# Batch 0's first pair: a mix's copies behind the second product, w_out's decoding behind the mix's step, v's second part one step at a time from group 3

## The chip, the cores and the metric

The kernel runs on one core of one Trainium2 chip. The metric is the device time of one execution in microseconds (us); a profiled execution's span runs from its first to its last instruction. TensorE is called PE, VectorE DVE, ScalarE ACT, GpSimd POOL and SyncE SP.

## The reference

Two stages follow each other. Channel attention over two batches of 6016 tokens and 256 channels: q and k are normalized over the tokens, `s = knᵀ qn / tau` is a 256 x 256 matrix for each batch, `a = softmax(s)`, and the result is `v @ a`. Then a feed-forward layer over all 12032 tokens, with 2048 hidden channels:

```python
    h = x @ w_in
    g = h * (1.0 / (1.0 + np.exp(-h)))
    return (g @ w_out).astype(np.float32)
```

## The kernel before

The kernel multiplies `a` into `w_in` first, one mixed weight for each batch, so that the hidden layer is a product of this weight with v. Each fp32 operand is split into two fp16 halves, hi and lo, and a product is made of three matmuls (lo x hi, hi x lo, hi x hi).

**Pairs and groups.** A *pair* is 1024 tokens (896 at a batch's end), in two halves of 512: six pairs per batch, twelve in all. In each pair there are eight *groups* i = 0..7, each for 256 of the 2048 hidden channels. A group would need eight products of 512 columns; by a Strassen-Winograd scheme `emit_pair_group` does it in seven, in three PSUM banks: y and x (L657 on), z, then y, x, x, x again. Between them ACT copies a bank (`copy`, L640: c5 and c1, then c2), DVE subtracts (`minus`, L645: g11, g12, g22), ACT applies silu (L651, the fourth straight from the last x), and `finish` splits the result into hl: ACT casts the high half (L147), DVE makes the low half (L148). The generator yields four times in a group, in *slots* 0 to 3: behind z, behind the second x, behind the third x, behind the last x.

**Output matmuls.** Each of the four hl of a group gives six output matmuls into bank o (`emit_out`, L595). They are issued a group late, one hl per slot, as the list `pending`. A pair's last ones are followed by the evictions of its four o banks (L614 on ACT, L618 on DVE), and the next pair's output matmuls take the same four banks.

**The mixed weights.** Group i's weights are wall[i], made by `mix(b, i)`: 12 matmuls into bank w (L419), two scaled copies on ACT (L427), three subtractions on DVE (L433, L437, L440), then a cast to the high half on ACT (L144) and the low half on DVE (L145). The first matmul of a group's first y reads the low half. In pair 0, wall[i+1] is made during group i, one step of the generator per slot (`nextmix`), and before it `decode_wi` decodes w_in's next part (L186 on ACT, L188 on DVE, split by L147 and L148).

**Other work in pair 0.** `prepare`, in groups 0 and 1, goes on with `prepare_out`, which loads, decodes (L182 on POOL, L186, L188) and bounds (L196) w_out, and with two steps of batch 1's scores (`sc`, L277). Until w_out's scale is there, group 2 is not issued. `scale_v(1)` prepares the second pair's v: two squares (L481), the scale, and fp16 sums of v's halves in tile m (ACT L147, DVE L148, 1024 columns at once where they can be).

**What sets the order.** Instructions are emitted with a priority (their place in the program) and the tile framework orders each engine's list. `mark` notes the last instructions emitted, and `background` puts what it emits behind those on ACT, DVE and PE. Each engine works its list off in order.

```python
                mark()
                if p == 0 and i < NI - 1:
                    nextmix = background(nextmix)
```

Of the kernel before, what the change touches and what calls it, by code (L numbers as in the profile page):

```python
# [30 lines left out]
def channel_attention_then_silu_ffn(ctx, tc, kq, qT, kT, vT, tau, w_in, w_out, outT):  # L31
# [43 lines left out]
    def small_psum(name):  # L75

        if early[0]:
            return ps_o.tile([P, 512], F32, tag="o", name=name)
        return ps_b.tile([P, 512], F32, tag="z", name=name)
# [61 lines left out]
    def split(src, hi, lo, s=None):  # L141

        if s is None:
            nc.scalar.copy(hi, src)  # L144
            nc.vector.tensor_tensor(out=lo, in0=src, in1=hi, op=ALU.subtract)  # L145
            return
        nc.scalar.activation(out=hi, in_=src, func=AF.Copy, scale=s)  # L147
        nc.vector.scalar_tensor_tensor(  # L148
            out=lo, in0=src, scalar=s, in1=hi, op0=ALU.mult, op1=ALU.subtract
        )  # L150
# [261 lines left out]
    def mix(b, i):  # L412

        aT, rows = mixer[b]
        w = small_psum("w") if b == 0 else ps_b.tile([P, 512], F32, tag="a", name="w")
        for cb in range(KC):
            for j, (u, y) in enumerate(((1, 0), (0, 1), (0, 0))):
                for db in range(KC):
                    nc.tensor.matmul(  # L419
                        w[:, cb * C : (cb + 1) * C], aT[:, u, db, cb * P : (cb + 1) * P],  # L420
                        wi[:, y, db, i * C : (i + 1) * C],
                        start=(cb + db + j == 0), stop=(j == 2 and db == KC - 1),
                        skip_group_check=True,
                    )
        x = st.tile([P, 8, P], F32, tag="sq", name="x", bufs=2)
        for cb in range(KC):
            nc.scalar.activation(  # L427
                out=x[:, cb : cb + 3 : 2],
                in_=w[:, cb * C : (cb + 1) * C].rearrange("p (a c) -> p a c", c=P),
                func=AF.Copy, scale=rows[:, cb : cb + 1],  # L430
            )
        yield
        nc.vector.tensor_tensor(  # L433
            out=x[:, S1 : S3 + 1], in0=x[:, A21 : A21 + 1].to_broadcast([P, 2, P]),
            in1=x[:, A22 : A11 + 1], op=ALU.subtract,
        )
        nc.vector.tensor_tensor(  # L437
            out=x[:, S2], in0=x[:, S1], in1=x[:, A11], op=ALU.subtract
        )
        nc.vector.tensor_tensor(out=x[:, S4], in0=x[:, S2], in1=x[:, A12], op=ALU.add)  # L440
        yield
        m = wall[:, i]
        for a, c in ((A22, S3), (S3, S4 + 1)) if b or i == 0 else ((A22, S4 + 1),):
            hi, lo = m[:, 0, a - 1 : c - 1], m[:, 1, a - 1 : c - 1]
            if b:
                nc.vector.tensor_copy(out=hi, in_=x[:, a:c])
                nc.vector.tensor_tensor(out=lo, in0=x[:, a:c], in1=hi, op=ALU.subtract)
            else:
                split(x[:, a:c], hi, lo)
            yield  # L450
        mixed[b, i] = m


    pairs = [(b, n, min(NT, N - n)) for b in range(B) for n in range(0, N, NT)]
    loaded, parts = {}, {}

    def load_v(p):
        if p >= len(pairs):
            return
        b, n, w = pairs[p]  # L460
        t = vp.tile([P, KC, NT], F32, tag="v", name="v_t", bufs=3)
        nc.sync.dma_start(
            t[:, :, :w], vT[:, b * N + n : b * N + n + w].rearrange("(k p) n -> p k n", p=P)
        )
        loaded[p] = t
# [219 lines left out]
    def steps(gen):  # L685

        while True:
            try:
                next(gen)
            except StopIteration as e:  # L690
                return e.value

    def spend(gen, n=1):
        for _ in range(n):
            if gen is None:
                return None
            try:
                next(gen)
            except StopIteration:
                return None  # L700
        return gen
# [71 lines left out]
    def traced():  # L773
        return nc.cur_bb.bb.instructions
# [13 lines left out]
    def behind(start, those, engines=GATED):  # L788

        for i in traced()[start:]:  # L790
            if i.engine in engines and i.engine in those:
                tc.add_manual_dep(
                    i, those[i.engine].name,
                    mybir.DependencyInfo(
                        mybir.DependencyClass.NoSync, mybir.DependencyReason.DATA
                    ),
                )
# [10 lines left out]
    with at(0):  # L808
# [11 lines left out]
        for g in range(len(groups[0])):  # L820
# [15 lines left out]
            if g == 9:  # L836
                vgen = scale_v(0)
# [16 lines left out]
    def mark():  # L854

        anchor.update(last_of())

    def background(gen, n=1):

        start = len(traced())  # L860
        gen = spend(gen, n)
        behind(start, anchor)
        return gen

    def decode_wi(j):
        x = yield from decode(None, raws[j])
        while "in" not in weights:
            yield
        split(x, *(wi[:, u, :, j * C : (j + 1) * C] for u in range(2)), weights["in"][0])
# [58 lines left out]
    def prepare():  # L928

        nonlocal filler  # L930
        for _ in range(2):
            if "out" not in weights:
                next(wout)
        filler = spend(filler, 2)
# [5 lines left out]
    for p, (b, n, w) in enumerate(pairs):  # L940
        vgen = None
        last = n + w == N and b + 1 < B
        if n + w == N - pairs[-1][2] and b + 1 < B:
            steps(sqgen)
            norms["go"] = True
        for i in range(NI):
            if i == (4 if p == 0 else 0) and p + 1 < len(pairs):
                load_v(p + 1)
                vgen = scale_v(p + 1)
            if p == 0:  # L950
                if i == 2:
                    while "out" not in weights:
                        prepare()
                    spend(wout)
                    early[0] = False
                if i < NI - 1:
                    for j in ((), (2,), (3,), (4, 5), (6, 7), (), ())[i]:
                        steps(decode_wi(j))
                    nextmix = mixes.pop(0)
            if b and (b, i) not in mixed:  # L960
                steps(mixes.pop(0))
            pending, ready[:] = ready[:], []
            if p == 0 and i == 1:
                held_back = pending
                pending = []
            if p == 0 and i == 2:
                pending = held_back + pending
            slot = 0
            for _ in emit_pair_group(p, i):
                if p == 0 and i < 2:  # L970
                    prepare()
                take = 2 if p == 0 and i > 2 and len(pending) > 4 - slot else 1
                for _ in range(take):
                    if pending:
                        emit_out(pending.pop(0))
                mark()
                if p == 0 and i < NI - 1:
                    nextmix = background(nextmix)
                if i >= 1 and vgen is not None and (
                    p == 0 or slot in ((0, 2) if not last else (0, 2, 3) if i > 4 else (2, 3))  # L980
                ):
                    vgen = background(vgen, 2 if p == 0 else 1)
                if filler is not None and b == 0 and (p or i >= 2):
                    if "go" not in norms or slot < 2:
                        filler = background(filler, 1)
                if p in (1, 2, 3) and sqgen is not None and slot == 1:
                    sqgen = background(sqgen) or iter(())
                if p and mixes and slot == 0:
                    if mixes[0] is old and background(mixes.pop(0), 2):
                        raise RuntimeError("a mix has more steps")  # L990
                if p and mixes and slot != 1:
                    old = mixes[0]
                    background(old)
                if p == 0 and 2 <= i < 5 and slot in (0, 2):
                    wout = background(wout)
                slot += 1
            if last:
                mixes.append(mix(b + 1, i))
            ready[:0] = pending
            if p == 0 and i < NI - 1:  # L1000
                if nextmix is not None:
                    steps(nextmix)
        if vgen is not None:
            steps(vgen)
# [32 lines left out]
```

## Time and profile before

| | |
|---|---|
| Runs, median of 3 | 1035.51 us (1035.3 to 1035.76) |
| The profiled execution | 1035.6 us, span 1033.8 us |
| PE busy | 1026.4 us, 99% of the span |
| ACT busy | 836.2 us, 81% |
| DVE busy | 716.2 us, 69% |
| POOL busy | 9.8 us, 1% |
| HBM read, written | 57.67 MB, 12.32 MB |

The profiled execution stands 1.8 us above its span, and within the runs' spread. Busy matmuls are pipelined, so that PE's 99% says that it seldom lacks work, not that it runs at its peak. Pair 0 begins at 63.3 us of the span, behind the loading of k and q, and its eight groups last until 176 us.

### The profile page before, as it was taken

The numbers are of one execution on the slowest core, as the hardware profiler recorded it, in microseconds if no ns is written. First come the engines' busy times: TensorE is split into PE (matmuls) and PEld (weight loads), VectorE is DVE, ScalarE is ACT, GpSimd is POOL, SyncE is SP. The second block draws the span as 40 slices with busy tenths as digits, with TensorE's granted clock in tenths as the row PEclk, the third lists the DMA queues.
The fourth block names the chain that finished last, engine by engine and source line by source line (L and its number), as shares of the span: only waits on it lengthen the run. The fifth ranks groups of instructions, "written<-read, shape, count | busy, mean of one in ns | idle before, by whom it ended". The sixth has DMA issues, their size and how long they took to land.

```text
span 1033.8 us, 13058 instructions
## 1 busy us (share of the span) xinstructions
PE 1026.4 (99%) x4942; PEld 519.7 (50%) x4942; DVE 716.2 (69%) x1229; ACT 836.2 (81%) x1342; POOL 9.8 (1%) x23
## 2 busy tenths in 40 slices
PE   9999999999999999999999999999999999999998
PEld 8877554444444444444555444444444444444554
DVE  5987676667667667767688767667667667667654
ACT  6677788889989889788778778778778778778876
POOL 1011000000000000000000000000000000000000
PEclk9999999999999999999999999999999999999999
DMA  9996420312313101100101100200200100100101
GB/s 371 396 399 207 131 85 38 102 42 94 100 45 98 60 1 40 43 1 22 62 1 42 36 1 1 82 1 1 77 1 1 41 1 1 41 1 0 42 1 36
DMA packets 25984, 70.82 MB, mean 69 GB/s; under 512 B 2498, under 2 KB 3650, under 8 KB 25922
## 3 DMA queue, kind: packets, MB, share of 16 engines
q1 hardware_dynamic: 25346, 68.84, 18.8%
q8 instruction: 38, 0.62, 0.3%
q10 hardware_dynamic: 432, 0.64, 0.2%
q0 software_dynamic: 144, 0.52, 0.1%
q14 instruction: 24, 0.20, 0.1%
HBM read 57.67 MB, written 12.32 MB: 68 GB/s over the span
## 4 chain that ended last, share of the span: by engine, by line
PE 89%; DVE 4%; ACT 3%; DMA 2%; issue 1%; DVEq 0%; SPq 0%; ACTq 0%
PE o L595 45%; PE x L634 22%; PE y L634 11%; PE z L634 5%; PE sc L277 4%; DMA kq_t<-in_kq 2%; PE w L419 1%; DVE wo L274 1%; DVE hl L148 1%; ACT g L651 1%; ACT hl L147 1%; DVE g L645 1%; PE idle L815 0%; ACT m L147 0%; ACT c L640 0%
## 5 line engine op out<-in xcount | busy, mean ns | idle before, releaser
L595 PE MATMUL o<-hl,wo 128*128 128x512 f16 (+1 forms) x2304 | 548.7, 375 | 0.0
L148 DVE SCALAR_TENSOR_TENSOR hl<-g,sg,hl 128x512 f16<-128x512 f32 (+1 forms) x384 | 282.5, 739 | 172.2 <-ACT hl L147 170.5
L595 PEld LDWEIGHTS <-wo 128*128 128x128 f16 x2304 | 225.5, 98 | 261.2
L634 PEld LDWEIGHTS <-wall 128*128 128x128 f16 x2016 | 196.6, 98 | 226.7 <-issue 3.0
L634 PE MATMUL x<-m,wall 128*128 128x512 f16 (+1 forms) x1152 | 306.2, 375 | 1.0 <-ACT c L640 0.7
L651 ACT ACTIVATE g<-g,alpha 128x512 f32<-128x512 f32 (+1 forms) x288 | 203.5, 707 | 118.2 <-DVE g L645 116.9
L147 ACT ACTIVATE hl<-g,sg 128x512 f16<-128x512 f32 (+1 forms) x384 | 271.5, 711 | 10.3
L634 PE MATMUL y<-m,wall 128*128 128x512 f16 (+1 forms) x576 | 153.1, 375 | 0.5 <-DVE wall L145 0.5
L640 ACT COPY c<-x 128x512 f32<-128x512 f32 (+1 forms) x192 | 110.6, 576 | 24.8 <-PE x L634 21.5
L645 DVE TENSOR_TENSOR g<-x,c 128x512 f32<-128x512 f32 (+1 forms) x96 | 65.2, 680 | 45.2 <-PE x L634 45.2
L645 DVE TENSOR_TENSOR g<-c,z 128x512 f32<-128x512 f32 (+1 forms) x96 | 64.9, 676 | 38.4 <-PE z L634 33.7
L277 PE MATMUL sc<-kq_t 128*128 128x256 f32 x376 | 86.9, 384 | 0.0
L645 DVE TENSOR_TENSOR g<-c,y 128x512 f32<-128x512 f32 (+1 forms) x96 | 64.7, 674 | 18.7 <-ACT c L640 18.4
L277 PEld LDWEIGHTS sc<-kq_t 128*128 128x128 f32 x376 | 71.5, 193 | 11.4 <-DMA kq_t<-in_kq 0.3
L634 PE MATMUL z<-m,wall 128*128 128x512 f16 (+1 forms) x288 | 76.5, 375 | 0.0
L651 ACT ACTIVATE g<-x,alpha 128x512 f32<-128x512 f32 (+1 forms) x96 | 63.4, 661 | 1.3 <-PE x L634 1.3
L640 ACT COPY c<-y 128x512 f32<-128x512 f32 (+1 forms) x96 | 54.7, 569 | 8.7 <-PE y L634 6.9
L147 ACT ACTIVATE m<-v_t,sv 128x512 f16<-128x512 f32 (+2 forms) x46 | 33.1, 726 | 3.9 <-DVE sv L123 3.0
L274 DVE TENSOR_TENSOR wo<-wo,sq 128x1024 f32<-128x1024 f32 (+1 forms) x24 | 27.7, 1156 | 10.3 <-ACT sq L272 9.2
L148 DVE SCALAR_TENSOR_TENSOR m<-v_t,sv,m 128x512 f16<-128x512 f32 (+2 forms) x46 | 34.7, 758 | 0.0
L148 DVE SCALAR_TENSOR_TENSOR m<-x,sv,m 128x512 f16<-128x512 f32 (+2 forms) x35 | 26.2, 753 | 8.7 <-ACT m L147 8.7
L272 ACT ACTIVATE sq<-kq_t 128x1024 f32<-128x1024 f32 (+1 forms) x24 | 23.6, 998 | 7.6 <-DMA kq_t<-in_kq 4.8
(132 smaller groups left out, 396.0 us busy)
## 6 DMA issues: line engine op xcount, KB each, us to landing
kq_t<-in_kq SPq DMA_DIRECT2D x39, 512.0 KB, 8.2
v_t<-in_vT SPq DMA_DIRECT2D x10, 1024.0 KB, 5.1
outT<-sb SPq DMA_DIRECT2D x40, 256.0 KB, 2.1
turned<-in_qT SPq DMA_DIRECT2D x10, 512.0 KB, 3.6
turned<-in_kT SPq DMA_DIRECT2D x10, 512.0 KB, 3.5
kq_t<-in_kq SPq DMA_DIRECT2D x14, 256.0 KB, 7.4
raw<-in_w_in SPq DMA_DIRECT2D x5, 512.0 KB, 9.8
wo<-in_w_out SPq DMA_DIRECT2D x4, 512.0 KB, 9.6
```

Of the source, the lines that this page charges most:

```text
L147: nc.scalar.activation(out=hi, in_=src, func=AF.Copy, scale=s)
L148: nc.vector.scalar_tensor_tensor(out=lo, in0=src, scalar=s, in1=hi, op0=ALU.mult, op1=ALU.subtract)
L272: nc.scalar.activation(out=sq[:, :n], in_=t[:, :n], func=AF.Square)
L274: nc.vector.tensor_tensor(out=a, in0=a, in1=sq[:, :n], op=ALU.add)
L277: nc.tensor.matmul(sc[:, cb, :], t[:, i, 0, cb * P : (cb + 1) * P], t[:, i, 1, :], start=(j + i == 0 and cb == 0), stop=(j + i == J - 1), ...
L419: nc.tensor.matmul(w[:, cb * C : (cb + 1) * C], aT[:, u, db, cb * P : (cb + 1) * P], wi[:, y, db, i * C : (i + 1) * C], start=(cb + db + j ...
L595: nc.tensor.matmul(o[:, :h], a[:, f, ee], hl[:, m, :h], start=(c == 1 and i == 0), stop=(c == NF and i == 2),)
L634: nc.tensor.matmul(bank[:, :h], wm[:, u, a - 1], m[:, y, x, :h], start=(first and j == 0), stop=(j == 2), skip_group_check=True,)
L640: nc.scalar.copy(t[:, :h], bank[:, :h])
L645: nc.vector.tensor_tensor(out=g[:, :h], in0=a[:, :h], in1=c[:, :h], op=ALU.subtract)
L651: nc.scalar.activation(out=g[:, :h], in_=src[:, :h], func=AF.Silu, scale=alpha)
```

## The change

Four edits, all of them for batch 0, and in pair 0 alone in effect. A mix with i > 0 gets one more yield, between its 12 matmuls and its copies: the copies come in slot 1, the subtractions in slot 2, the split in slot 3. `prepare` comes behind the mix's step, no longer ahead of the output matmuls. The load and the scaling of pair 1's v begin in group 3, not 4. Its steps come one at a time in slots 0, 2 and 3, not two at a time in every slot.

```diff
@@ -422,6 +422,8 @@
                         start=(cb + db + j == 0), stop=(j == 2 and db == KC - 1),
                         skip_group_check=True,
                     )
+        if b == 0 and i:
+            yield
         x = st.tile([P, 8, P], F32, tag="sq", name="x", bufs=2)
         for cb in range(KC):
             nc.scalar.activation(
@@ -944,7 +946,7 @@
             steps(sqgen)
             norms["go"] = True
         for i in range(NI):
-            if i == (4 if p == 0 else 0) and p + 1 < len(pairs):
+            if i == (3 if p == 0 else 0) and p + 1 < len(pairs):
                 load_v(p + 1)
                 vgen = scale_v(p + 1)
             if p == 0:
@@ -967,8 +969,6 @@
                 pending = held_back + pending
             slot = 0
             for _ in emit_pair_group(p, i):
-                if p == 0 and i < 2:
-                    prepare()
                 take = 2 if p == 0 and i > 2 and len(pending) > 4 - slot else 1
                 for _ in range(take):
                     if pending:
@@ -976,10 +976,12 @@
                 mark()
                 if p == 0 and i < NI - 1:
                     nextmix = background(nextmix)
-                if i >= 1 and vgen is not None and (
-                    p == 0 or slot in ((0, 2) if not last else (0, 2, 3) if i > 4 else (2, 3))
+                if p == 0 and i < 2:
+                    prepare()
+                if i >= 1 and vgen is not None and slot in (
+                    (0, 2, 3) if p == 0 or last and i > 4 else (2, 3) if last else (0, 2)
                 ):
-                    vgen = background(vgen, 2 if p == 0 else 1)
+                    vgen = background(vgen, 1)
                 if filler is not None and b == 0 and (p or i >= 2):
                     if "go" not in norms or slot < 2:
                         filler = background(filler, 1)
```

How the engines' lists move is shown at three places; from L425 on, a line of the changed kernel has a number higher by two.

**ACT, the end of group 0**, before and then changed. `x<-w,rows` are the mix's copies, `wall<-x` is the mix's cast, `g<-x,alpha` the silu of the last x, `t<-wo` and `t<-wall` are decoding casts for w_out.

```order
L427 ACTIVATE x<-w,rows 128x2x128 x2
L640 COPY c_634<-x 128x512
L186 CAST t<-wo 128x512
L651 ACTIVATE g<-g,alpha 128x512
L147 ACTIVATE hl<-g,sg 128x512
L651 ACTIVATE g<-g,alpha 128x512
L147 ACTIVATE hl<-g,sg 128x512
L144 CAST wall<-x 128x896
L651 ACTIVATE g<-x,alpha 128x512
L186 CAST t<-wall 128x512
L147 ACTIVATE hl<-g,sg 128x512
```

```order
L642 COPY c_631<-x 128x512
L429 ACTIVATE x<-w,rows 128x2x128 x2
L186 CAST t<-wo 128x512
L653 ACTIVATE g<-g,alpha 128x512
L147 ACTIVATE hl<-g,sg 128x512
L653 ACTIVATE g<-g,alpha 128x512
L147 ACTIVATE hl<-g,sg 128x512
L653 ACTIVATE g<-x,alpha 128x512
L186 CAST t<-wall 128x512
L147 ACTIVATE hl<-g,sg 128x512
L144 CAST wall<-x 128x896
```

The cast into wall stood ahead of the last x's silu; now it stands behind it, behind a decoding cast and behind the last hl cast. The mix's copies stand behind c2.

**DVE, the end of group 6**, before and then changed. `wall<-x,wall` is the low half of wall[7], `m<-v_t,sv,m` belongs to pair 1's v.

```order
L645 TENSOR_TENSOR g<-c_1431,y 128x512
L148 SCALAR_TENSOR_TENSOR hl<-g,sg,hl 128x512
L433 TENSOR_TENSOR x<-x 128x256
L437 TENSOR_TENSOR x<-x 128x128
L440 TENSOR_TENSOR x<-x 128x128
L645 TENSOR_TENSOR g<-x,c_1387 128x512
L148 SCALAR_TENSOR_TENSOR hl<-g,sg,hl 128x512
L145 TENSOR_TENSOR wall<-x,wall 128x896
L148 SCALAR_TENSOR_TENSOR hl<-g,sg,hl 128x512 x2
```

```order
L647 TENSOR_TENSOR g<-x,c_1375 128x512
L148 SCALAR_TENSOR_TENSOR hl<-g,sg,hl 128x512
L435 TENSOR_TENSOR x<-x 128x256
L148 SCALAR_TENSOR_TENSOR m<-v_t,sv,m 128x1024
L439 TENSOR_TENSOR x<-x 128x128
L442 TENSOR_TENSOR x<-x 128x128
L148 SCALAR_TENSOR_TENSOR hl<-g,sg,hl 128x512 x2
L525 TENSOR_TENSOR x<-x,v_t 128x512
L145 TENSOR_TENSOR wall<-x,wall 128x896
L647 TENSOR_TENSOR g<-c_1476,z 128x512
```

Wall's low half stood ahead of the group's last two hl; now it stands behind them, behind a low half of v over 1024 columns (which before stood in group 5) and behind a subtraction for v.

**PE, group 7 from its z on**, before and then changed, with buffer numbers: `m_293` is pair 0's v, `wall` the weights, `o_886<-hl_1422` an output matmul for group 6's first hl.

```order
L634 MATMUL z_1490<-m_293,wall_87 128x512
L634 LDWEIGHTS wall_87
L634 MATMUL z_1490<-m_293,wall_87 128x512
L595 LDWEIGHTS wo_86
L595 MATMUL o_886<-hl_1422,wo_86 128x512
L595 LDWEIGHTS wo_86
L595 MATMUL o_886<-hl_1422,wo_86 128x512
L595 LDWEIGHTS wo_86
```

```order
L636 MATMUL z_1482<-m_293,wall_87 128x512
L636 LDWEIGHTS wall_87
L636 MATMUL z_1482<-m_293,wall_87 128x512
L636 LDWEIGHTS wall_87
L636 MATMUL y_1471<-m_293,wall_87 128x512
L636 LDWEIGHTS wall_87
L636 MATMUL y_1471<-m_293,wall_87 128x512
L636 LDWEIGHTS wall_87
```

Before, group 6's output matmuls stood between z and the second y. Now they stand ahead of group 7: counted over the list, 168 output matmuls come before group 7's first product, and 144 before. Behind z the second y follows at once.

## Rows read from the trace of the kernel before

**Rows 1.** The page: busy times, and the granted clock in tenths over 40 slices.

```profile
PE 1026.4 (99%) x4942; PEld 519.7 (50%) x4942; DVE 716.2 (69%) x1229; ACT 836.2 (81%) x1342; POOL 9.8 (1%) x23
PEclk9999999999999999999999999999999999999999
```

**Rows 2.** Timeline of PE, 60 to 165 us: start us, us, instruction, count [idle before, releaser].

```profile
65.25 1.03 PE L277 MATMUL sc<-kq_t 128*128 128x256 f32 x4
...
73.34 0.81 PE L634 MATMUL x<-m,wall 128*128 128x512 f16 x3
73.98 2.75 PE L277 MATMUL sc<-kq_t 128*128 128x256 f32 x12
77.21 0.82 PE L634 MATMUL y<-m,wall 128*128 128x512 f16 x3 [0.47 <-DVE wall L145]
...
92.58 0.22 PE L98 MATMUL pb<-spread,ones 128*128 128x128 bf16 x1
...
96.14 0.81 PE L634 MATMUL y<-m,wall 128*128 128x512 f16 x3
...
98.08 1.46 PE L595 MATMUL o<-hl,wo 128*128 128x512 f16 x6
99.38 1.47 PE L419 MATMUL w<-wi,aT 128*128 128x256 f16 x12
```

**Rows 3.** Timeline of ACT, v's cast at 150 us and the pairs' change at 181 us.

```profile
150.28 1.15 ACT L147 ACTIVATE m<-v_t,sv 128x1024 f16<-128x1024 f32 x1
...
181.16 1.06 ACT L242 ACTIVATE sq<-turned 128x1024 f32<-128x1024 f32 x1
...
182.21 0.71 ACT L651 ACTIVATE g<-g,alpha 128x512 f32<-128x512 f32 x1
...
186.55 0.68 ACT L614 ACTIVATE sb<-o,back 128x512 f32<-128x512 f32 x1
187.12 0.58 ACT L640 COPY c<-y 128x512 f32<-128x512 f32 x1
```

**Rows 4.** Timeline of DVE, groups 0 and 1.

```profile
65.15 0.75 DVE L148 SCALAR_TENSOR_TENSOR wi<-t,swi,wi 128x512 f16<-128x512 f32 x1 [0.72 <-ACT wi L147]
...
75.47 0.68 DVE L196 TENSOR_REDUCE ao<-wall 128x1 f32<-128x512 bf16 x1
76.07 1.08 DVE L145 TENSOR_TENSOR wall<-x,wall 128x896 f16<-128x896 f32 x1
...
85.27 0.28 DVE L93 TENSOR_SCALAR spread<-ident,ao 128x128 bf16<-128x128 f32 x1
```

**Rows 5.** Timeline of ACT, the end of group 0.

```profile
74.64 0.92 ACT L144 CAST wall<-x 128x896 f16<-128x896 f32 x1
75.47 0.68 ACT L651 ACTIVATE g<-x,alpha 128x512 f32<-128x512 f32 x1
76.05 0.77 ACT L186 CAST t<-wall 128x512 f16<-128x512 bf16 x1
76.67 0.72 ACT L147 ACTIVATE hl<-g,sg 128x512 f16<-128x512 f32 x1
```

**Rows 6.** Timeline of DVE, v's sums in group 5.

```profile
151.35 0.68 DVE L523 TENSOR_TENSOR x<-x,v_t 128x512 f32<-128x512 f32 x1
...
152.16 1.28 DVE L148 SCALAR_TENSOR_TENSOR m<-v_t,sv,m 128x1024 f16<-128x1024 f32 x1
```

**Rows 7.** Timeline of PE: group 7's first y, pair 1's first output, group 2 of pair 1.

```profile
166.23 0.81 PE L634 MATMUL y<-m,wall 128*128 128x512 f16 x3
...
187.60 1.46 PE L595 MATMUL o<-hl,wo 128*128 128x512 f16 x6
...
195.37 0.81 PE L634 MATMUL y<-m,wall 128*128 128x512 f16 x3
```

**Rows 8.** Waits of PE over the span: us in total, times, longest us.

```profile
PE idle L815 <- DVE ones L53: 1.1, 1, 1.1
PE x L634 <- ACT c L640: 0.7, 2, 0.4
```

## The prediction

> **What bounds the kernel now.** I read the page's busy times first, then the windows of 10 us, then the timeline of each engine from 60 to 202 us, where everything the change moves stands. The page shows TensorE (PE) busy for 99% of the span, ScalarE (ACT) for 81%, and the granted clock at its upper level, 2.4 GHz, in every slice [rows 1]. So a microsecond is lost or won only where PE waits. In the timeline of PE the reader sees matmuls that start one behind the other: a product of three matmuls takes 0.65, six output matmuls 1.30, twelve of a mix 1.31, twelve score matmuls 2.59 [rows 2] (a row's length less 0.16, which is its drain: 73.34, 0.81 long, next 73.98). The wait that the change is about is at 77.21, the first product of group 1, which waited 0.47 for the low half of wall[1] [rows 2].
>
> I call the seven products of a group by their banks: first y, first x, z, second y, second x, third x, last x. I compare three legs between first products: group 0 to group 2, group 2 to group 7, group 7 to group 2 of the next pair. On each, I take the new order of the three engines and put to each instruction the duration of its row; one that starts behind another follows after about 0.1 less than the row's length (186.55, 0.68 long, next 187.12) [rows 3]. PE's matmuls are the same in kind and number, so the sum is one of waits.
>
> **Leg 1, group 0 to group 2: +1.3 us.** In group 0 two edits cancel. The mix's 12 matmuls now follow z at 65.25 without the score matmuls ahead of them, and wait for the low half of wi, done at 65.90 [rows 2, 4]: they end 0.46 late. The third x no longer waits for its copy behind the two mix copies, which gives about as much back. So the last x stands where it stood, at 73.34 [rows 2]. From there the new order on ACT is: silu of the last x, a decoding cast, the hl cast, and only then wall's cast, which before ran ahead of that silu, at 74.64 [rows 5]. The result is there at 74.15; the third x, issued at 70.93, has its subtraction done by 72.89 and its silu by 73.65, so ACT is at its hl cast until 74.30; silu 74.30 to 74.97; cast from 74.87; hl cast 75.49 to 76.21; wall's cast 76.11 to 77.03. On DVE two reductions (0.60 each) and the low half of hl (0.66, the kind of 65.15) come first, until 77.46, then wall's low half, 1.08 [rows 4], ends at 78.54. PE's cover is the last x and 12 score matmuls: until 76.57 [rows 2]. So the first y comes at 78.56, not 77.21: +1.35. All of PE's list is queued behind this y, and ACT's next copy waits for its result. In group 1 the same walk finds wall[2] ready at 92.7, while score matmuls last until 97.4 (before: 96.14 [rows 2]); nothing more is lost, and 1.28 stays. Decoding of w_out moves behind the mix's step: casts, reductions and DVE's merges come up to one step later, its DMAs stand where they stood on SP and POOL, and POOL's memsets keep their order. I cost this at nothing because its end, the spread of w_out's bound at 85.27, has until the matmul pb at 92.58 [rows 2, 4]; without that cover each step is 0.6 to 0.7 us. Bounds of the leg: if the reductions run while DVE would idle, 0.9; if a cast waits for its memset, 2.0.
>
> **Leg 2, groups 2 to 7: +1.9 us.** The first y of each group now waits for a chain that starts at the last x before it: 0.81 to the result, silu 0.7, a decoding cast 0.62 in groups 2 and 3, hl cast 0.72, wall's cast 0.92, wall's low half 1.08. The order lets PE run score matmuls and output matmuls meanwhile, taken from the next group's share. From the last x: group 2, chain 4.68 against a cover of 0.65 + 1.30 + 0.86 + 8 x 0.216 = 4.53; group 3, 4.69 against 4.53; group 4, 4.96 against 0.65 + 17 x 0.216 = 4.32, since the third x's subtraction and the bits of v's scale stand in the way; group 5, 6.38 against 0.65 + 25 x 0.216 = 6.05, with v's cast over 1024 columns (1.15) and its low half (1.28) ahead of wall's two [rows 3, 6]; group 6, 6.5 against 0.65 + 20 x 0.216 = 4.97, with the same v cast ahead of the third x's silu, and v's subtraction (0.68 [rows 6]) ahead of wall's low half. These waits are 0.15, 0.16, 0.64, 0.33 and 1.53, together 2.8; in group 4 v's two squares hold up the copy of the first x, 0.2: 3.0. Before, the leg took 70.09 (96.14 to 166.23) [rows 2, 7], and its matmuls take 35 x 0.648 + 144 x 0.216 + 5 x 1.31 + 40 x 0.216 + 0.06 = 69.0, so 1.1 was waiting, and goes. Net +1.9. Bounds: 0.5 with waits half as long, 4.0 with each of five chains 0.4 longer.
>
> What this leaves behind counts more: counted in the order, 168 output matmuls now stand ahead of group 7, before 144. PE enters group 7 with 24 x 0.216 = 5.2 us of its reserve used up.
>
> **Leg 3, group 7 to group 2 of the next pair: +3.7 us.** PE has to pass through this leg 5.2 us faster than before to be level again, and ACT decides. The first output matmul of the new pair needs a bank that ACT empties with its second eviction. Before, that eviction ended at 187.23 and the matmul started at 187.60 [rows 3, 7]: 0.37 to spare. Now PE has 16 products and 24 output matmuls from group 7's first y to there, 16 x 0.648 + 24 x 0.216 = 15.55 us. ACT's list in the same stretch is 6 copies x 0.47, 8 silu (6 x 0.62, 2 x 0.57), 8 hl casts x 0.62, one square 1.05, 2 evictions x 0.57 [rows 3, 5], and v's last two casts, 1.05 and 0.62, which were done long before: 16.5 us. It begins 0.83 after the first y, idles about 1.45 where it waits for copies' subtractions on DVE, and its last result takes 0.1 more: 18.9. DVE's eviction of the second bank comes 0.2 to 0.3 later. PE waits 3.7 us in all, the largest piece, 2.7, at that bank. After it, the rest goes back to back. Bounds: 1.9 if ACT never idles (0.83 + 16.5 + 0.1 - 15.55), 5.9 if it idles 0.8 before each of five silu.
>
> **The sum.** 1.3 + 1.9 + 3.7 = 6.9. The profiled execution took 1035.6 (span 1033.8), 0.1 above the median of the runs, 1035.51. 1035.6 + 6.9 = **1042.5 us**. The rest of the program keeps its order on PE and runs parallel.
>
> **The rivals.**
> - *ACT's relief wins (faster).* Before, v's two squares and casts fell into groups 4 and 5; spread over five groups ACT has room, and PE's waits there go. It decides at wall's low half: if that starts less than 3.4 us after the last x, the cover of 4.5 us hides it everywhere, the order has no need of its reserve, and what is won is leg 2's 1.1 and leg 1's two waits, 0.4 for a copy [rows 8] and 0.5 for wall [rows 2], 2.0: 1033.6. For it: ACT is the second busiest engine [rows 1]. Against: the ACT order puts silu, hl and wall in line, 0.81 + 0.67 + 0.72 + 0.92 = 3.1 without any cast between or hl work on DVE. Chance 0.05. The Trainium skill, "Perfetto Trace Analysis", section "Optimization Strategy", speaks for this rival: where regimes differ, interleaving them may help. No row here shows a gain by that.
> - *Only the boundaries bite evenly (no change).* If ACT catches up in the o-filled stretches and leg 3 ends at 0, while legs 1 and 2 cost no more than the 2.0 that goes, the time is 1035 to 1037. Against it stands the bank's 0.37 of slack. Chance 0.08.
> - *The clock falls too.* A wait of 2.7 us is longer than any of PE's here (1.1 at the start [rows 8]), and the trace shows no stretch at 1.2 GHz [rows 1]. If the clock fell for half a group of 9.7 us, the work in it would take twice as long: +4.9, 1047.4; bounds 0 and 9.7. Chance 0.05. The Trainium skill, "TensorE: Matmul & The Clock Gate", Part 1, says that PE drops to half clock after idling. By that rule the change would cost more than the sum.
> - That the change doesn't do what it says is excluded by the order: wall's cast does stand behind the last silu.
>
> **How the numbers follow.** The forecast has 0.82. About 0.2% (2.1 us) is what a measurement of this kernel can tell from no change, so slower is 0.82 + 0.05 = 0.87, the same 0.08, faster 0.05. The range: the lower bounds sum to 0.9 + 0.5 + 1.9 = 3.3, 1038.9, taken to 1038.5; the upper to 2.0 + 4.0 + 5.9 = 11.9, but hardly all three at once, so I stop at 1046.5.
>
> **What would show it.** Right: the waits of PE name wall's low half six times, with group 1's first y near 78.5 and group 7's near 174.6; the first output matmul of pair 1 waits some 2.7 us for an ACT eviction; group 2 of pair 1 starts near 202, not 195.37 [rows 7]. Wrong: group 7's first y before 172.5, or PE without a wait at that bank; or a granted clock below 1.

## The result and the profile after

The change makes the kernel slower: 1040.79 us, median of 5 runs (1040.75 to 1041.2), against 1035.64 (1035.3 to 1035.76) beside it; ratio 1.0052, interval 1.0041 to 1.0063. That is 5.15 more, where 6.9 was forecast. The profiled execution took 1040.95, span 1039.2.

The page of the changed kernel, busy times and granted clock, against [rows 1]:

```profile
PE 1028.4 (99%) x4942; PEld 517.9 (50%) x4942; DVE 715.4 (69%) x1229; ACT 834.5 (80%) x1342; POOL 9.9 (1%) x23
...
PEclk9999999999999999999999999999999999999999
```

ACT and DVE are busy for nearly as long as before, and the clock stays at its upper level. PE's share still reads 99%: the loss has to be looked for in PE's starts. The timeline of PE (start, length, engine, line, operation, operands, count, and in brackets the idle time and its releaser), against [rows 2, 7]; the rows from 73.95 to 175.42 that read y are first products of groups 1 to 7, 200.54 is that of group 2 of pair 1:

```profile
73.95 2.75 PE L277 MATMUL sc<-kq_t 128*128 128x256 f32 x12
78.62 0.82 PE L636 MATMUL y<-m,wall 128*128 128x512 f16 x3 [1.92 <-DVE wall L145]
...
97.54 0.81 PE L636 MATMUL y<-m,wall 128*128 128x512 f16 x3
...
113.99 0.82 PE L636 MATMUL y<-m,wall 128*128 128x512 f16 x3
...
132.61 0.82 PE L636 MATMUL y<-m,wall 128*128 128x512 f16 x3
...
148.21 0.82 PE L636 MATMUL y<-m,wall 128*128 128x512 f16 x3 [0.41 <-DVE wall L145]
...
161.75 0.82 PE L636 MATMUL y<-m,wall 128*128 128x512 f16 x3 [0.18 <-DVE wall L145]
...
172.36 2.93 PE L597 MATMUL o<-hl,wo 128*128 128x512 f16 x12 [0.81 <-ACT hl L147]
175.42 0.82 PE L636 MATMUL y<-m,wall 128*128 128x512 f16 x3
...
191.69 1.03 PE L597 MATMUL o<-hl,wo 128*128 128x512 f16 x4
...
193.25 1.96 PE L597 MATMUL o<-hl,wo 128*128 128x512 f16 x7
...
200.54 0.81 PE L636 MATMUL y<-m,wall 128*128 128x512 f16 x3
```

| | before | after | output matmuls moved ahead | more waiting |
|---|---|---|---|---|
| leg 1, group 0 to 2 | 63.30 to 96.14: 32.84 | 63.31 to 97.54: 34.23 | 0 | 1.4 |
| leg 2, group 2 to 7 | 96.14 to 166.23: 70.09 | 97.54 to 175.42: 77.88 | 24 x 0.216 = 5.18 | 2.6 |
| leg 3, group 7 to 2 of pair 1 | 166.23 to 195.37: 29.14 | 175.42 to 200.54: 25.12 | 24 fewer | 1.2 |

Together 5.2: the difference of the medians, and all but 0.2 of that of the two profiled executions (1040.95 - 1035.6 = 5.35). The waits of PE (line waited for, us in total, times, longest), against [rows 8]:

```profile
PE y L636 <- DVE wall L145: 2.5, 3, 1.9
PE o L597 <- ACT hl L147: 0.8, 1, 0.8
```

Before, wall's low half had one wait of 0.47 [rows 2]. Now it stands first with 2.5 in three named waits, and there are some shorter ones that this view doesn't name: 113.99 starts 0.24 late and 132.61 0.25, seen by adding up the rows ahead of them.

### The profile page after: what moved, and what is told of

Same layout as the page of the kernel before. It is cut to its first block, busy times and chain, and to the rows that moved or that the text cites. A ratio compares the mean times of both kernels' runs of the same rounds, so it can differ in the third digit from the quotient of the medians.

```text
span 1039.2 us, 13060 instructions
## 1 busy us (share of the span) xinstructions
PE 1028.4 (99%) x4942; PEld 517.9 (50%) x4942; DVE 715.4 (69%) x1229; ACT 834.5 (80%) x1342; POOL 9.9 (1%) x23
## 4 chain that ended last, share of the span: by engine, by line
PE 85%; DMA 6%; ACT 5%; DVE 4%; issue 0%; SPq 0%
PE o L597 42%; PE x L636 22%; PE y L636 11%; PE z L636 5%; DMA kq_t<-in_kq 4%; PE sc L277 3%; ACT g L653 2%; ACT hl L147 1%; PE w L419 1%; DVE hl L148 1%; DMA raw<-in_w_in 1%; DMA wall<-in_w_out 1%; DVE wall L145 1%; ACT c L642 1%; DVE g L647 1%; DVE m L148 0%
## 5 line engine op out<-in xcount | busy, mean ns | idle before, releaser
L647 DVE TENSOR_TENSOR g<-c,y 128x512 f32<-128x512 f32 (+1 forms) x96 | 64.7, 674 | 19.1 <-ACT c L642 18.9
```

Source lines behind the costliest of these rows:

```text
L647: nc.vector.tensor_tensor(out=g[:, :h], in0=a[:, :h], in1=c[:, :h], op=ALU.subtract)
```

## The experiments

**Theory T** (called Y in the later runs): the extra yield puts wall's split into slot 3, where its cast is behind the last x's silu and hl cast on ACT and its low half behind hl's on DVE, and PE runs out of work ahead of the first y. The rivals: **V**, v's earlier casts are what delays ACT; **P**, it is the decoding of w_out behind the mix's step.

**1. One part alone.** The extra yield alone:

```diff
+        if b == 0 and i:
+            yield
         x = st.tile([P, 8, P], F32, tag="sq", name="x", bufs=2)
```

> The kernel before with the mix's extra yield alone. Theory (late split: wall's cast and low half stand behind the last x's silu and hl, so that PE runs dry at the first y of a group): this edit carries nearly all of the cost, 1039.0 to 1041.3 us, group 2 of pair 1 starts 3.5 to 5.5 us later than 195.4, and PE's waits name wall's low half. Rival V (v's casts, moved ahead of wall's split in groups 5 and 6, make the cost): at most half of the 5.2 us, 1036.5 to 1038.2. Rival P (prepare's later step makes leg 1's 1.4): group 2 of pair 0 starts at 96.1 as before.

Measured: 1041.25, 1041.38, 1043.04 and 1043.41 against 1035.44. The two lower runs are 5.8 and 5.9 above, the top of what theory T allowed or a little over; the two higher ones belong to the last section. In the profiled execution, one of the higher, group 2 of pair 1 starts at 202.87, 7.5 later than before, 1.6 of it by what the last section shows. The yield alone costs more than the whole change. Its waits are not all at wall: only group 1's first y has a named wait for wall's low half (2.3), and ahead of group 6 PE waits for hl casts instead (1.0 in two named waits).

`prepare` behind the mix's step alone:

```diff
-                if p == 0 and i < 2:
-                    prepare()
...
                     nextmix = background(nextmix)
+                if p == 0 and i < 2:
+                    prepare()
```

> The kernel before with prepare behind the mix's step alone. Theory (late split): within 0.6 us of before, 1035.0 to 1036.2, group 2 of pair 0 at 96.1 +- 0.4. Rival P (prepare's later step makes leg 1's loss): 1036.6 to 1037.4, group 2 of pair 0 at 97.3 to 97.7.

Measured: 1035.64, ratio 1.0002 (0.9992 to 1.0012). P falls.

v's two edits alone (from group 3, one step at a time in slots 0, 2 and 3):

> The kernel before with v's two edits alone (from group 3, one step in slots 0, 2 and 3). Theory (late split): no loss, perhaps the 0.5 us of waits in groups 4 and 5 goes: 1034.6 to 1036.0. Rival V (v's later casts make the cost of groups 5 to 7 and of the next pair's start): 1037.5 to 1039.5.

Measured: 1036.07, ratio 1.0006 (0.9996 to 1.0015), just over the 1036.0 that the theory allowed. V falls as the cause of 5; and there is no gain either. The timeline of this kernel in group 4, ACT, then DVE, then PE:

```profile
131.82 1.04 ACT L481 ACTIVATE m<-v_t 128x1024 f32<-128x1024 f32 x1
...
132.86 0.56 ACT L640 COPY c<-y 128x512 f32<-128x512 f32 x1
...
133.94 0.69 DVE L645 TENSOR_TENSOR g<-c,z 128x512 f32<-128x512 f32 x1 [0.79 <-ACT c L640]
...
134.68 1.47 PE L419 MATMUL w<-wi,aT 128*128 128x256 f16 x12 [0.37 <-DVE g L645]
```

v's second square keeps ACT until 132.86, so the copies of the first y and x start late, DVE's subtraction comes at 133.94, and the mix's matmuls wait for it.

Both together, without the yield:

> The change without the mix's extra yield. Theory (late split): about the kernel before, 1034.4 to 1036.0, no wait of PE for wall's low half longer than 0.6 us. Rivals V and P: 1037.5 to 1040.0.

Measured: 1036.2, ratio 1.0008 (0.9998 to 1.0017), as v's edits alone, and 0.2 over the theory's range. No named wait of PE is for wall in it; in the starts, the first y's of groups 1 and 6 come 0.26 and 0.28 late behind wall's low half.

**2. What v's edits and prepare do beside the yield.** The yield and v's edits, then the yield and prepare:

> The change without the move of prepare: the extra yield and v's two edits. Theory Y (the extra yield costs 5.8 by itself, and v's edits give a part of it back because they free ACT ahead of wall's cast in groups 4 to 6): 1040.3 to 1041.0, as all edits together. Rival P (what is given back, about 0.5, comes from the move of prepare): 1041.2 to 1041.9, as the yield alone or above. If PE falls to half clock behind the wait at group 1's first y, as in two runs of the yield alone, single runs lie 1.8 higher.

Measured: 1040.68, 1040.83, 1041.01 and 1042.35 against 1035.42.

> The extra yield and prepare behind the mix's step, without v's edits. With prepare moved, the wait at group 1's first y is 1.9 as with all edits, not 2.3 as with the yield alone. Theory Y: 1041.0 to 1041.5 in every run (v's edits, left out, gave 0.4 to 0.5 back). If the fall to half clock behind that wait hangs on its length, no run lies 1.5 or more above the fastest; if it comes by chance behind a wait of either length, some do.

Measured: 1041.41 (1041.34 to 1041.51, 5 runs) against 1035.52. So v's edits give back 0.5 to 0.7 of what the yield costs, and prepare next to nothing. In the timeline of the kernel without v's edits leg 2 costs 78.31 - 70.09 - 23 x 0.216 = 3.25, not 2.6.

**3. One group's mix, and the others.** The whole change with the yield for wall[1] alone, and for wall[2] to wall[7] alone:

```diff
-        if b == 0 and i:
+        if (b, i) == (0, 1):
```

> The whole change, but the extra yield in the mix of wall[1] alone, which is made in group 0. Theory Y (each leg pays for its own waits): leg 1's 1.4 stays, legs 2 and 3 are as with v's edits without the yield (+0.5): 1037.0 to 1037.6. Rival R (what is lost at group 1's first y is won back behind it, since PE's lists hold slack there, and the cost of the change is that of the later groups): 1035.8 to 1036.3.

Measured: 1037.42 (1037.25 to 1037.69) against 1035.52, ratio 1.0019 (1.001 to 1.0028).

```diff
-        if b == 0 and i:
+        if i > 1 and b == 0:
```

> The complement: the whole change, with the extra yield in the mixes of wall[2] to wall[7] and not in that of wall[1]. Theory Y: leg 1 is as before, legs 2 and 3 cost 2.6 + 1.2: 1039.0 to 1039.7. Rival R: 1040.4 to 1041.0, as the whole change. Rival F (the 1.9 at group 1 puts all that follows out of step, and the later waits come from that): 1035.8 to 1036.6.

Measured: 1039.54 (1039.49 to 1039.55), ratio 1.0039 (1.0025 to 1.0052). 1.9 + 4.0 = 5.9; both contain v's 0.5, and less that once it is 5.4, near the 5.15 of the change. Each group pays for its own wait, and rivals R and F fall. PE in the kernel with wall[1] alone, and in the one with wall[2] to wall[7]:

```profile
78.74 0.82 PE L636 MATMUL y<-m,wall 128*128 128x512 f16 x3 [1.93 <-DVE wall L145]
```

```profile
146.79 0.82 PE L636 MATMUL y<-m,wall 128*128 128x512 f16 x3 [0.41 <-DVE wall L145]
...
160.34 0.82 PE L636 MATMUL y<-m,wall 128*128 128x512 f16 x3 [0.19 <-DVE wall L145]
...
170.94 2.93 PE L597 MATMUL o<-hl,wo 128*128 128x512 f16 x12 [0.81 <-ACT hl L147]
```

The first has the change's wait at group 1 and no later named wait for wall (group 6's first y starts 0.29 late behind it, as with v's edits alone: 0.28); the second starts group 1 only 0.26 late and then shows the waits of the whole change to within 0.01.

**4. The split moved or shortened.** The whole change with the subtractions and the split in one step again:

```diff
         nc.vector.tensor_tensor(out=x[:, S4], in0=x[:, S2], in1=x[:, A12], op=ALU.add)
-        yield
+        if b or i == 0:
+            yield
```

> The whole change, but the subtractions and the split of a mix stand in one step again (slot 2), so that wall's cast is ahead of the last silu on ACT at the ends of groups 1 to 4; the copies stay behind the second product. At the ends of groups 0, 5 and 6 the cast stays behind the last silu and hl. Theory Y (it is wall's place behind the last x's work that costs): the four waits of 0.24, 0.25, 0.57 and 0.34 for wall's low half at groups 2 to 5 go, and with them some 1.4; group 1's 1.9 stays: 1038.9 to 1040.0. Rival M (it is the later copies and the score matmuls and output matmuls that changed places, not the split): no change against all edits together, 1040.5 to 1041.2.

Measured: 1040.43 (1040.16 to 1040.57) against 1035.42, 5.0 above where the change is 5.15 above: a miss for theory Y, and just under rival M's range. PE's timeline, then ACT's at the end of group 6, then ACT, DVE and PE at the end of group 2:

```profile
137.01 1.47 PE L419 MATMUL w<-wi,aT 128*128 128x256 f16 x12 [0.38 <-DVE g L648]
...
147.53 0.82 PE L637 MATMUL y<-m,wall 128*128 128x512 f16 x3
...
161.37 0.82 PE L637 MATMUL y<-m,wall 128*128 128x512 f16 x3 [0.34 <-DVE wall L145]
...
175.04 0.82 PE L637 MATMUL y<-m,wall 128*128 128x512 f16 x3
...
171.22 1.32 ACT L147 ACTIVATE hl<-g,sg 128x512 f16<-128x512 f32 x2
172.45 0.93 ACT L144 CAST wall<-x 128x896 f16<-128x896 f32 x1
```

```profile
110.58 0.94 ACT L144 CAST wall<-x 128x896 f16<-128x896 f32 x1
111.42 0.68 ACT L654 ACTIVATE g<-x,alpha 128x512 f32<-128x512 f32 x1
...
111.55 1.09 DVE L145 TENSOR_TENSOR wall<-x,wall 128x896 f16<-128x896 f32 x1 [0.23 <-ACT wall L144]
...
111.53 1.03 PE L277 MATMUL sc<-kq_t 128*128 128x256 f32 x4
```

Of the four short waits one has gone (group 4's); the first y's at 147.53, 161.37 and 175.04 still start 0.23, 0.50 and 0.28 late. For the last two, wall's cast still stands behind two hl casts at the ends of groups 5 and 6. But at the ends of groups 2 and 4 it stands ahead of the last x's silu, as was intended, and PE waits all the same: 0.23 at 147.53, and 0.30 at group 3's first y (112.70), where PE's score matmuls last until 112.39 and wall's low half until 112.64. There it is not the place behind the silu that costs; the copies, which still come one slot later, are the likely reason, but no run moves them alone. And the mix's matmuls get a wait of 0.38, as in the kernel with v's edits alone. So this run doesn't tell the theories apart; the next one tells whether the split is on PE's path at all. (Its profiled execution started pair 0 at 63.68, 0.37 later than the change's, which no part of it explains; by PE's rows from there on it lost 0.7 less than the change.)

The whole change with wall's split in two pieces, 512 columns first, which the first y reads:

```diff
-        for a, c in ((A22, S3), (S3, S4 + 1)) if b or i == 0 else ((A22, S4 + 1),):
+        for a, c in ((A22, S3), (S3, S4 + 1)):
...
-            yield
+            if b or i == 0 or c > S3:
+                yield
```

> The whole change, with the order of steps as it is, but wall's split made in two pieces (512 columns, which the first y reads, then 384), as for the first mix. Theory Y: the chain from the last x to the first y is shorter by some 0.3 on ACT (a cast of 512 columns takes 0.62, not 0.92) and 0.4 on DVE (0.66, not 1.08), 0.7 at each of six ends of groups: 1.92, 0.24, 0.25, 0.57, 0.34 and 1.54 become 1.2, 0, 0, 0, 0 and 0.85, that is 2.8 less of waiting; less what two more instructions on each engine take in each group: 1037.8 to 1039.3. Rival M (the split is not what costs): 1040.5 to 1041.5.

Measured: 1038.74 (1038.68 to 1038.77) against 1035.42: 3.3 above where the change is 5.15 above, inside theory Y's range; rival M, by which a shorter split gains nothing, falls. ACT, DVE and PE at group 1's start, then PE at the starts of groups 3 and 7:

```profile
76.00 1.02 ACT L144 CAST wall<-x 128x512 f16<-128x512 f32 x2
...
76.71 0.76 DVE L148 SCALAR_TENSOR_TENSOR hl<-g,sg,hl 128x512 f16<-128x512 f32 x1
77.37 1.17 DVE L145 TENSOR_TENSOR wall<-x,wall 128x512 f16<-128x512 f32 x2
...
78.12 0.82 PE L637 MATMUL y<-m,wall 128*128 128x512 f16 x3 [1.53 <-DVE wall L145]
```

```profile
113.11 0.82 PE L637 MATMUL y<-m,wall 128*128 128x512 f16 x3 [0.19 <-DVE wall L145]
...
172.01 0.82 PE L637 MATMUL y<-m,wall 128*128 128x512 f16 x3 [0.24 <-DVE wall L145]
```

The wait fell by 0.39 there, not by 0.7: DVE is at hl's low half until 77.37 and begins wall's no earlier than in the change (77.48), so ACT's shorter first cast saves nothing and only DVE's shorter piece counts. The other places are not as theory Y had them either. It put the four short waits at nothing; by the starts they are 0.36, 0.14, 0.57 and 0.47, together 1.5 where the change has 1.4, with fewer output matmuls ahead of these y's than in the change (5 for 8 at group 3, 14 for 17 at group 5). The gain lies elsewhere: 0.2 in leg 1, 0.9 in leg 2, where 1.1 is won ahead of group 7, and 0.7 in leg 3.

**5. A version to beat both.** The same two pieces in the kernel before, with prepare moved and without it moved:

> The kernel before with wall's split in two pieces for every mix and with prepare behind the mix's step; no extra yield, v's edits left out. Theory Y: the wait of 0.47 for wall's low half at group 1's first y goes, and nothing else waits for wall: 1035.0 to 1035.4 (0.1 to 0.5 below the kernel before). Rival: the two extra instructions per group on ACT and DVE delay copies and subtractions by what they add in fixed time: 1035.6 to 1036.2.

Measured: 1035.53 (1035.32 to 1035.86) against 1035.42, ratio 1.0001 (0.9992 to 1.001): above theory Y's range and below its rival's.

> The kernel before with wall's split in two pieces for every mix and nothing else changed, prepare ahead of the output matmuls as before. Theory: the wait of 0.47 at group 1's first y goes, and the mix's matmuls do not wait for wi (0.3 and 0.2 with prepare moved): 1034.9 to 1035.2. Rival: what is won at group 1 is waited for elsewhere in group 1, as with prepare moved: 1035.3 to 1035.7.

Measured: 1035.7 (1035.44 to 1035.99) against 1035.52, ratio 1.0001 (0.9993 to 1.001), as the rival has it. The wait of 0.47 goes in both, and its time does not come back. PE with nothing but the two pieces:

```profile
75.57 0.81 PE L635 MATMUL y<-m,wall 128*128 128x512 f16 x3
...
79.74 0.38 PE L419 MATMUL w<-wi,aT 128*128 128x256 f16 x2 [0.34 <-ACT wi L147]
```

Score matmuls that stood ahead of the first y now stand behind it; the y comes at 75.57, 1.64 earlier, and the mix's matmuls, sooner there, wait for the decoded wi. Group 2 starts at 96.11, before at 96.14: leg 1 has another limit right behind the one removed. No version here beats the kernel before.

## Why the prediction was right, and where it was not

**Leg 1, +1.3: right.** Against the working, the last x's silu came at 74.30 (74.30), the hl cast at 75.50 (75.49), wall's cast at 76.12 (76.11), and the first y at 78.62 (78.56). The rows of ACT and DVE in the changed kernel, against [rows 4, 5]:

```profile
74.30 0.67 ACT L653 ACTIVATE g<-x,alpha 128x512 f32<-128x512 f32 x1
74.87 0.76 ACT L186 CAST t<-wall 128x512 f16<-128x512 bf16 x1
75.50 0.71 ACT L147 ACTIVATE hl<-g,sg 128x512 f16<-128x512 f32 x1
76.12 0.93 ACT L144 CAST wall<-x 128x896 f16<-128x896 f32 x1
```

```profile
75.63 1.27 DVE L196 TENSOR_REDUCE ao<-wall 128x1 f32<-128x512 bf16 x2
76.82 0.74 DVE L148 SCALAR_TENSOR_TENSOR hl<-g,sg,hl 128x512 f16<-128x512 f32 x1
77.48 1.08 DVE L145 TENSOR_TENSOR wall<-x,wall 128x896 f16<-128x896 f32 x1
```

wall's cast has 0.93 and its low half 1.08 behind all of hl's work, and PE's cover ends at 76.54. That 1.4 stays lost is shown by the run with wall[1] alone.

**Leg 2, +1.9: the mechanism right, the size 0.7 short.** The waits behind groups 2 to 5, worked out as 0.15, 0.16, 0.64 and 0.33, are 0.24, 0.25, 0.57 and 0.34 at the first y's of groups 3 to 6; the one at group 7, 1.53, is 1.54, most of it ahead of the output matmuls at 172.36, which wait for the hl cast and not for wall. The prediction looked for wall's low half six times in PE's waits; the view names it three times, the short ones are in the starts alone. Together 2.94 against 2.8. What was missed are waits of 0.07 to 0.15 inside groups 4 to 6 (seven, 0.7 in sum, where 0.2 was put down). The waiting of the kernel before in this leg, 1.1, comes out as put down. The bounds, 0.5 and 4.0, hold it.

**Leg 3, +3.7: mis-sized; it measured 1.2.** The step that failed is "The first output matmul of the new pair needs a bank that ACT empties with its second eviction". ACT in the changed kernel, with the two evictions:

```profile
190.08 0.67 ACT L616 ACTIVATE sb<-o,back 128x512 f32<-128x512 f32 x1
...
193.67 0.68 ACT L616 ACTIVATE sb<-o,back 128x512 f32<-128x512 f32 x1
```

The output matmuls at 191.69 start right behind z (191.04 and 0.65), without a wait, after the first eviction and before the second: they take the bank of ACT's first eviction. The 2.7 at the bank of the second did not come, which the prediction had named as a sign that it is wrong. ACT itself ran as worked out: its second eviction ends at 194.35, 18.9 after the first y. Its bank is first needed by the fifth of the seven matmuls at 193.25, behind four others, the x and four more: 15.55 + 0.65 + 8 x 0.216 = 17.9 of work. 18.9 - 17.9 = 1.0 is then what the same walk gives, and the row of seven is 1.96 long, 0.29 more than 7 x 0.216 + 0.16; the rest of the 1.0 had been waited away before. In the starts of the single matmuls of that row, half of the 0.29 is the fifth's wait for this eviction, the other half the third's for an hl cast. The slack before was no 0.37 either: the matmul at 187.60 [rows 7] had the bank of the first eviction, since PE's last wait for ACT ahead of it, at 186.30, is over before the second eviction begins at 186.55 [rows 3]. ACT's first eviction in the kernel before:

```profile
183.58 0.67 ACT L614 ACTIVATE sb<-o,back 128x512 f32<-128x512 f32 x1
```

The term's own lower bound, 1.9, did not hold it. That the sum still came out 1.7 above the measured 5.2 and not further off is in part luck: leg 3 is 2.5 too high and leg 2 is 0.7 too low.

**The reserve** is then repaid: the 24 matmuls taken out of leg 3 save 4.0 of their 5.2 there. What is left of them is leg 3's 1.2.

**The parts costed at nothing.** Prepare: right, 0.2 alone, which its interval doesn't tell from nothing. v's edits were counted in leg 2 with 0.2 in group 4; alone they cost 0.5 at that place. Beside the yield they save 1.1 ahead of group 6's first y, where PE waits 1.45 in the kernel with the yield and prepare and 0.35 in the changed one, and give back 0.5 of it elsewhere in the leg.

**The rivals.** ACT's relief did not win: no kernel with v's edits is faster, and of the first y's only group 2's finds wall ready. For the rival of no change, leg 3 came nearer to its 0 than to 3.7, but legs 1 and 2 cost 4.0 more than before, where by it their waits would not exceed the 2.0 that goes. The clock did not fall in the changed kernel.

## What to carry to other kernels

Before a step is moved one slot later, ask behind which of the last product's work its instructions then queue on each engine, and set that chain against the work that PE has until the consumer: here chains of 4.7 to 6.5 us met 3.2 to 6.1 of cover. Work that PE draws ahead from a later group to fill a wait is not lost, but it is missing there, and what that costs depends on how soon the other engines' lists are done; so a wait has to be followed to the leg's end before it is counted. When the reuse of a buffer decides, find out which buffer of the set is taken: here it was that of the first eviction, not of the second.

## What was not expected of the hardware

With the yield alone, PE waits 2.29 at group 1's first y. Of its four executions two ran 1.8 and 2.2 above the fastest. The profiled one is one of them; PE's timeline and the windows of 2 us (busy time and count of each engine, the granted clock, DMA share, GB/s):

```profile
73.78 2.75 PE L277 MATMUL sc<-kq_t 128*128 128x256 f32 x12
78.81 1.46 PE L636 MATMUL y<-m,wall 128*128 128x512 f16 x3 [2.29 <-DVE wall L145]
80.07 1.49 PE L636 MATMUL x<-m,wall 128*128 128x512 f16 x3
81.35 1.19 PE L636 MATMUL z<-m,wall 128*128 128x512 f16 x3
```

```profile
76.00:78.00 2.00, 0.53 (x3) 0.12 (x1) 2.00 (x5) 1.87 (x3) 0.00 (x0) 1.00 1.04 408
78.00:80.00 2.00, 1.19 (x3) 0.43 (x4) 2.00 (x4) 0.75 (x2) 0.00 (x0) 0.67 1.02 408
80.00:82.00 2.00, 2.00 (x6) 0.76 (x5) 1.22 (x2) 1.11 (x3) 0.53 (x1) 0.50 0.28 113
82.00:84.00 2.00, 2.00 (x13) 1.54 (x12) 1.35 (x3) 1.48 (x3) 0.00 (x0) 0.97 0.00 0
```

The clock is at its upper level until 78, falls between 78 and 80, where the wait ends at 78.81, is at half, 1.2 GHz, between 80 and 82, and is back near 82. y, x and z take 1.46, 1.49 and 1.19 where they took 0.81 each; the first product of group 2 comes 20.53 after that of group 1, where 18.92 is usual, so this costs 1.6. It was the third rival, priced at 4.9 for half a group; it lasted three products. The Trainium skill, "TensorE: Matmul & The Clock Gate", Part 1, says that PE drops to half clock after idling, and this row agrees. With waits of 2.3 (the yield alone, the yield with v's edits), three of eight executions lie 1.7 to 2.2 above their kernel's fastest, with a mean clock of 0.998; with waits of 1.9 or less none of 24 does (the changed kernel, the yield with prepare, the split with the subtractions, wall[1] alone). Whether the length of the wait alone decides was not tried: in both of the former kernels prepare also stands where it stood before.
